# Token transposes on the DMA queue, scales on VectorE, and weights prepared one expert ahead in a fused attention, routing and two-level expert kernel

## Chip, cores and metric

The kernel runs on one core of a Trainium2 chip. The metric is device time in microseconds, the median of several executions; lower is better. TensorE multiplies and transposes through PSUM, VectorE (DVE) and ScalarE (ACT) read PSUM and SBUF, GpSimd (POOL) issues the gathers and scatters, and SyncE (SP) issues the other DMAs.

## What is computed

```python
def _attn_ref(r, k, v, w, u):                      # 4 batches, 8 heads, 768 steps, head size 48
    for t in range(S):
        cur = np.einsum('bhd,bhe->bhde', u[None] * kt, vt)
        y[:, :, t] = np.einsum('bhd,bhde->bhe', rt, state + cur)
        state = w[None, :, :, None] * state + np.einsum('bhd,bhe->bhde', kt, vt)

def _moe_ref(x, w_gate, w1, w2):                   # x 3072x384, 8 experts, F = 1024
    # each token goes to one expert, best logit first, at most 384 tokens per expert
    h = np.maximum(x[mask] @ w1[e], 0.0)
    out[mask] = h @ w2[e]

def _moe2_ref(x, w1, w2, w3, w_out):               # 384 -> 768 -> 384
    h = np.maximum(np.maximum(x @ w1, x @ w2), x @ w3)
    return h @ w_out
```

The attention's output, 3072 rows of 384, is routed, goes through the chosen expert's two matrices, and then through the second layer, whose four matrices arrive as 64-bit floats.

## The kernel before

The kernel has three stages, one behind the other on every engine. The instructions of an engine stand in the order in which the program is written; nothing is reordered.

The attention (class `Attention`) runs 24 steps of 128 tokens. The routing (class `Routing`) is three rounds of a threshold search, `settle`, which writes the row numbers `ids`, a first gather of token rows by POOL, and a branch (`tc.If` at L1297) to a fallback that isn't taken. The experts' stage (`Experts.run`) follows.

For each expert there are 384 tokens in three groups of 128, and four products, each with operands split into a high and a low f16 part, so that every block is three matmuls. `first` makes the hidden layer (8 blocks of 9 matmuls), `second` the expert's output (3 blocks of 24), `third` the second layer's three branches (6 groups of 27) and `fourth` the final product (3 blocks of 18). Each matmul has 384 columns. `turn` transposes the gathered tokens: nine f32 transposes on TensorE into PSUM (L786), after which ACT writes the high part (L798) and DVE the low part (L799).

Weights are prepared beside this by a feed (`Feed`), a list of small items with estimated costs. A matrix of an expert (`weight(e, 0)` or `weight(e, 1)`) is loaded in two blocks of 768 KB, looked at (four sums of squares on ACT, L569), scaled, and split into high parts (ACT, L612) and low parts (DVE, L615). A 64-bit matrix (`double(i)`: 0, 1 and 2 are the layer's branches, 3 is its output matrix) comes in three blocks; for each of these its words are put together on DVE (L657, L658, L665, L672) before the looks and the splits (L693, L696). A load waits for one of four slots, in the order of the list.

A scale is one power of two per matrix. `Scales.spread` gets it from a column of 128 maxima in two items: `turn` transposes the column on TensorE (L395) and reduces the row on DVE (L397), and `share` multiplies the result by a row of ones on TensorE (L401), from whose PSUM tile `powering` works out the scale in some five small DVE operations.

In the attention the feed holds both matrices of experts 0 and 1 and the doubles 0 and 1, spread evenly over the steps (costs 9.0 and 9.3 for an expert's two matrices and 14.8 for a double: 66.2 in all). After it comes a second feed: double 2, then the matrices of expert 2, double 3, and the rest. In the experts' stage `side(time)` runs items at a pace worked out from what is left and when it is due, and `flush(tag)` runs all that are still missing up to a tag.

The order of the products before is: first 0, second 0, first 1, second 1, and then for each expert e `third(e)` with `first(e + 2)` and `turn(e + 3)` between its groups, `second(e + 2)` ahead of its last group, and `fourth(e)`. So the first layer runs two experts ahead of the second.

Of the kernel before, what the change touches and what calls it, by code (L numbers as in the profile page):

```python
# [22 lines left out]
DM = H * D  # L23
# [354 lines left out]
class Scales:  # L378


    def __init__(self, tc, pool, K):
        self.nc, self.pool, self.K, self.n, self.psum = tc.nc, pool, K, 0, None
# [5 lines left out]
    def spread(self, peak, then):  # L388
# [15 lines left out]
        return [turn, share]  # L404

# [53 lines left out]
class Feed:  # L459


    SLOTS, AHEAD = 4, 6
# [53 lines left out]
    def take(self, tag, budget, slot=None, time=1.0, apart=1.0):  # L516
# [3 lines left out]
        while self.left(tag) and self.spare > 0.3:  # L520
            pe = self.items[self.at][2]
            if pe and (self.now < self.ready or slot not in (None, pe)):
# [11 lines left out]
class Experts:  # L534
# [4 lines left out]
    def __init__(self, ctx, tc, K, w1, w2, vs, wo, x_dram, out):  # L539
# [4 lines left out]
        self.fix = ctx.enter_context(tc.tile_pool(name="fixed", bufs=1))  # L544
        self.sc = Scales(tc, ctx.enter_context(tc.tile_pool(name="scales", bufs=1)), K)
# [16 lines left out]
    def peak(self, x):  # L562
        p = self.sc.tile()
        self.nc.vector.tensor_reduce(p, x, AX.X, OP.max)
        return p

# [3 lines left out]

    def weight(self, e, which):

        nc = self.nc
        st = {}
# [16 lines left out]
        def peak():  # L591
            st["peak"] = self.peak(st["peaks"])

        def scale(top):
            st["s"], st["f"] = self.sc.power(top, 3, square=True)
# [11 lines left out]

        def split(n):
            def go():
                if n < len(parts):  # L610
                    raw, (hi, _) = part(*parts[n])
                    nc.scalar.activation(hi, raw, AF.Copy, scale=st["s"])  # L612
                if n:
                    raw, (hi, lo) = part(*parts[n - 1])
                    nc.vector.scalar_tensor_tensor(lo, raw, st["s"], hi, op0=OP.mult, op1=OP.subtract)  # L615
# [5 lines left out]
        turn, share = self.sc.spread(lambda: st["peak"], scale)  # L621
        return ([(look(j), False, [blocks[j // 2]], 0.9) for j in range(4)] + [(peak, False, blocks, 0.2)]
                + [(turn, 4, blocks, 0.2), (share, 2, blocks, 0.8)]
                + [(split(n), False, uses(n), 0.6 + 0.3 * which) for n in range(len(parts) + 1)])

    def double(self, i):
# [6 lines left out]
        st, bits = {}, {}  # L633
# [7 lines left out]
        def magnitude(j):  # L641
            a = bits[j] = self.wp.tile([128, 768], I32, name="da", bufs=2)
            nc.scalar.activation(a.bitcast(F32), pair(j)[1].bitcast(F32), AF.Abs, scale=65536.0)
# [5 lines left out]
        def shift(j):  # L649
            def go():  # L650
                total(j - 1)
                if j == 0:
                    magnitude(0)
                    st["x"] = self.room(i)
                    st["peaks"] = self.fix.tile([128, nb], F32, name=f"peaks{i}")
                x = bits[j].bitcast(F32)
                nc.vector.tensor_scalar(x, x, 2.0, None, op0=OP.max)  # L657
# [3 lines left out]
        def low(j):  # L661
            def go():
                if j + 1 < nb:
# [12 lines left out]
        def last():  # L676
            total(nb - 1)

        def peak():
            st["peak"] = self.peak(st["peaks"])  # L680

        def scale(top):
            st["s"], f = self.sc.power(top, 2, square=True, field=self.vf[:, i:i + 1] if i < 3 else None)
            if i == 3:
                self.wof = f
# [13 lines left out]
        turn, share = self.sc.spread(lambda: st["peak"], scale)  # L699
        near = [[blocks[j]] + blocks[j + 1:j + 2] for j in range(nb)]  # L700
        return ([(f(j), False, b, 1.1) for j in range(nb)
                 for f, b in ((shift, blocks[j:j + 1]), (low, near[j]), (sign, blocks[j:j + 1]))]
                + [(last, False, [], 0.1), (peak, False, [], 0.2), (turn, 4, [], 0.2), (share, 2, [], 0.8)]
                + [(split(j), False, [], 0.9) for j in range(nb + 1)])

# [5 lines left out]
    def common(self):  # L711
# [6 lines left out]
        self.vlow, self.ratio = low, [s[:, i:i + 1].bitcast(F32) for i in range(3)]  # L718

# [54 lines left out]
    def turn(self, e, blocks=False):  # L774
# [6 lines left out]

        def flip(n):
            ps = self.psum.tile([128, CAP], F32, name="px", bufs=3)
            for m in range(3):
                a, j = (n, m) if blocks else (m, n)
                nc.tensor.transpose(ps[:, m * 128:(m + 1) * 128], self.XG[e % 2][a][:, j * 128:(j + 1) * 128], K.identf)  # L786
            tiles.append(ps)

        if blocks:
            flip(0)  # L790
        for n in range(3):
            if n + blocks < 3:
                flip(n + blocks)
            ps = tiles[n]
            hi, lo = (xt[:, t, :, n * 128:(n + 1) * 128] if blocks else xt[:, t, n] for t in range(2))
            if blocks:
                ps = ps.rearrange("p (j n) -> p j n", j=3)
# [40 lines left out]
    def second(self, e, between=lambda j: None):  # L838
# [10 lines left out]
        pk = sc.tile()  # L849
        nc.vector.tensor_reduce(pk, part, AX.X, OP.max)  # L850

        def halve(top):
            s, f = sc.power(top, 3)
# [531 lines left out]
```

## Time and profile before

| | us |
|---|---|
| median of 3 runs | 733.47 |
| lowest and highest | 732.11 to 737.27 |
| profiled execution, its own time | 732.94 |
| span of the profiled execution | 731.2 |
| TensorE busy | 680.0 (93%) |
| VectorE busy | 411.7 (56%) |
| ScalarE busy | 322.1 (44%) |
| GpSimd busy | 238.6 (33%) |

The span runs from the first to the last instruction of the one execution that was profiled; what lies around it is 732.94 - 731.2 = 1.74 us. Busy shares are means over stages with different limits: the attention ends at about 193 us, the routing at about 230 us, and the experts' stage fills the rest.

### The profile page before, as it was taken

The page shows a single profiled execution, that of the slowest core. Times are in us where ns is not written, and L with a number is a line of the kernel's source. Part 1 is how long each engine was busy: PE and PEld are TensorE (multiplying, and loading weights), DVE is VectorE, ACT ScalarE, POOL GpSimd, SP SyncE. Part 2 cuts the span into 40 slices and gives each one's busy share as a digit, 9 for nine tenths or more (in the row PEclk, how much of TensorE's full clock was granted, in tenths as well). Part 3 has the DMA queues.
Part 4 walks back from the last instruction along what each step waited for, and adds up shares of the span by engine and source line. Part 5 has one row for each costly group of instructions (what it writes and reads, how often), then busy time and mean ns, then how long its engine had stood idle before and what let it go on. Part 6 is the DMA issues. An engine that isn't in the chain of part 4 may idle for free.

```text
span 731.2 us, 14572 instructions
## 1 busy us (share of the span) xinstructions
PE 680.0 (93%) x5891; PEld 456.6 (62%) x5891; DVE 411.7 (56%) x954; ACT 322.1 (44%) x657; POOL 238.6 (33%) x264
## 2 busy tenths in 40 slices
PE   5898888999748999999999999999999999999996
PEld 4687667788636755555665666666566665666663
DVE  6779989788673767865453453453535344332120
ACT  3454343454313576655553554544555343232221
POOL 5889777787004200210220220221121021121222
PEclk8999998799756999999999999999999999999999
DMA  5976745562404222421230230321202000000000
GB/s 157 308 230 194 241 138 181 187 199 72 151 1 134 90 85 86 162 87 44 77 119 12 109 118 1 112 83 44 91 30 87 0 33 1 1 34 1 33 1 32
DMA packets 37962, 68.86 MB, mean 94 GB/s; under 512 B 4608, under 2 KB 25216, under 8 KB 37888
## 3 DMA queue, kind: packets, MB, share of 16 engines
q1 hardware_dynamic: 34816, 58.42, 25.0%
q0 software_dynamic: 3072, 9.44, 3.8%
q8 instruction: 48, 0.79, 0.4%
q14 instruction: 26, 0.21, 0.1%
HBM read 58.41 MB, written 9.44 MB: 93 GB/s over the span
## 4 chain that ended last, share of the span: by engine, by line
PE 61%; DVE 3%; issue 2%; ACT 1%; DMA 1%; POOL 1%; POOLq 0%; ACTq 0%; DVEq 0%
PE pg L807 28%; PE ps L807 22%; PE px L893 8%; PE px L401 1%; DVE w L615 1%; PE px L786 1%; DMA stage<-in_moe_w_out_dram 1%; ACT w L612 0%; DVE xt L799 0%; DVE top L877 0%; PE px L395 0%; POOL out_dram L898 0%; DVE x2s L857 0%; POOL gt L880 0%; DVE ht L835 0%
## 5 line engine op out<-in xcount | busy, mean ns | idle before, releaser
L807 PE MATMUL pg<-x2s,v 128*128 128x384 f16 x1296 | 216.8, 326 | 0.0
L807 PEld LDWEIGHTS <-v 128*128 128x128 f16 x1296 | 126.5, 98 | 83.2
L807 PEld LDWEIGHTS <-w 128*128 128x128 f16 x1242 | 115.7, 98 | 70.9 <-issue 1.9
L880 POOL TENSOR_TENSOR gt<-top,gt 128x384 f16<-128x384 f32 x48 | 45.6, 951 | 342.4 <-ACT gt L879 301.5
L877 DVE SCALAR_TENSOR_TENSOR top<-pg,sc,top 128x384 f32<-128x384 f32 x96 | 59.3, 618 | 125.4 <-PE pg L807 122.9
L807 PE MATMUL ps<-ht,w 128*128 128x384 f16 x576 | 95.6, 326 | 0.0
L807 PE MATMUL ps<-xt,w 128*128 128x384 f16 (+1 forms) x540 | 88.5, 317 | 0.8 <-DVE ht L835 0.6
L879 ACT ACTIVATE gt<-top 128x384 f16<-128x384 f32 x48 | 25.1, 523 | 139.3 <-DVE top L877 139.3
L615 DVE SCALAR_TENSOR_TENSOR w<-stage,sc,w 128x512 f16<-128x512 f32 (+1 forms) x80 | 74.2, 950 | 7.4 <-ACT w L612 7.3
L893 PE MATMUL px<-wo,gt 128*128 128x384 f16 x432 | 72.6, 326 | 0.0
L612 ACT ACTIVATE w<-stage,sc 128x512 f16<-128x512 f32 (+1 forms) x80 | 60.8, 797 | 9.6 <-DVE sc L430 9.2
L893 PEld LDWEIGHTS <-gt 128*128 128x128 f16 x432 | 41.8, 98 | 27.0
L569 ACT ACTIVATE junk<-stage 128x768 bf16<-128x768 f32 x64 | 53.4, 835 | 2.8 <-DMA stage<-in_moe_w_dram 2.2
L835 DVE SCALAR_TENSOR_TENSOR ht<-ps,ht 128x384 f16<-128x384 f32 x56 | 30.6, 554 | 32.6 <-ACT ht L834 32.6
L263 ACT ACTIVATE junk<-x 128x384 bf16<-128x384 f32 x24 | 12.6, 523 | 69.5 <-DVE x L262 67.7
L847 DVE TENSOR_REDUCE part<-ps 128x1 f32<-128x384 f32 x24 | 13.4, 556 | 51.4 <-ACT x L846 51.4
L226 PE MATMUL pA<-rt,kt 64*128 64x128 f32 x384 | 34.3, 314 | 7.8 <-DVE am L229 7.5
L898 POOL DMA_INDIRECT out_dram<-o,ids x24 | 23.4, 974 | 44.6 <-ACT o L896 44.6
L226 PEld LDWEIGHTS pA<-rt,kt 64*128 64x128 f32 x384 | 28.4, 212 | 14.3 <-DVE am L229 9.8
L229 DVE TENSOR_TENSOR am<-pA,mask 128x512 f32<-128x512 f32 x48 | 30.7, 680 | 8.9 <-PE pA L226 8.9
L875 ACT ACTIVATE top<-pg,sc 128x384 f32<-128x384 f32 x48 | 27.8, 579 | 16.6 <-PE pg L807 16.2
L202 POOL TENSOR_TENSOR bv<-v,bon 128x384 f32<-128x384 f32 x24 | 23.1, 964 | 31.0 <-DVE bon L200 28.5
(229 smaller groups left out, 916.8 us busy)
## 6 DMA issues: line engine op xcount, KB each, us to landing
stage<-in_moe_w_dram SPq DMA_DIRECT2D x41, 768.0 KB, 4.9
kn<-in_k_dram SPq DMA_DIRECT2D x24, 192.0 KB, 4.6
rn<-in_r_dram SPq DMA_DIRECT2D x24, 192.0 KB, 4.1
v<-in_v_dram SPq DMA_DIRECT2D x24, 192.0 KB, 3.1
rt<-in_rt_dram SPq DMA_DIRECT2D x48, 96.0 KB, 3.2
x_rows<-x SPq DMA_DIRECT2D x24, 192.0 KB, 2.6
stage<-in_moe_w_out_dram SPq DMA_DIRECT2D x3, 768.0 KB, 4.1
xg<-x_rows,ids POOLq DMA_INDIRECT x24, 4.6
```

Of the source, the lines that this page charges most:

```text
L226: nc.tensor.matmul(pa[s][:, j, :], kt[FULL[s], j * C:(j + 1) * C], rt[FULL[s], j * C:(j + 1) * C], start=True, stop=True, skip_group_check ...
L229: nc.vector.tensor_mul(am[:, s], pa[s], self.mask[:, None, :].to_broadcast([128, NP, C]))
L569: self.nc.scalar.activation(self.K.junk, x, AF.Square, accum_out=total)
L612: nc.scalar.activation(hi, raw, AF.Copy, scale=st["s"])
L615: nc.vector.scalar_tensor_tensor(lo, raw, st["s"], hi, op0=OP.mult, op1=OP.subtract)
L807: nc.tensor.matmul(p[:, rows], w[:, wi, k, cols], x[:, xi, k, rows], start=k == 0 and wi + xi == 0, stop=k == kb - 1 and xi == 1, skip_gro ...
L835: nc.vector.scalar_tensor_tensor(h[:, 1, f], p, 0.0, h[:, 0, f], op0=OP.max, op1=OP.subtract)
L875: nc.scalar.activation(t, p, AF.Copy, scale=self.ratio[i])
L877: nc.vector.scalar_tensor_tensor(t, p, self.ratio[i], top, op0=OP.mult, op1=OP.max)
L879: nc.scalar.activation(gt[:, 0, g], top, AF.Copy)
L880: nc.gpsimd.tensor_sub(gt[:, 1, g], top, gt[:, 0, g])
L893: nc.tensor.matmul(p, gt[:, gi, g, a * 128:(a + 1) * 128], self.WO[:, wi, g, :], start=g == 0 and gi + wi == 0, stop=g == self.KG - 1 and ...
```

## The change

Four things change.

1. `Scales.around` replaces `spread` in the experts' stage: the column is transposed on DVE in four 32x32 blocks, reduced, turned back with a broadcast, and copied twice; no TensorE instruction is left in it. In the attention the old way stays (`early`).
2. `turn` of experts 1 to 7 splits the gathered rows first, from SBUF, on ACT and DVE, and three transposing DMAs on SP's queue (`dma_start_transpose`, one for each group of 128 tokens, 192 KB) bring high and low parts into place. Expert 0 keeps the nine transposes on TensorE.
3. In the loop over experts `third(e)` now has `first(e + 1)` and `second(e + 1)` in it, and for e = 0 none; due times follow. Double 3 is due before `fourth(0)`, which now comes directly behind `third(0)`.
4. `weight(1, 1)` leaves the attention's feed (56.9 is left of 66.2) and opens the second feed. Its four looks run in the first two rounds of the routing, its scale behind the first gather, and its splits in the experts' stage. `Feed.chain` puts the looks (or the words) of the next matrix ahead of, or between, the scale and splits of the one before.

```diff
+    def around(self, peak, powers, kind):
...
+        def collect():
+            peak(a[:, :1])
+            for q in range(4):
+                nc.vector.transpose(b[:32, 32 * q:32 * q + 32], a[32 * q:32 * q + 32])
+            nc.vector.tensor_reduce(c[:32, :1], b[:32], AX.X, OP.max)
+
+        def share():
+            nc.vector.transpose(d[:32], c[:32, :1].to_broadcast([32, 32]))
+            nc.vector.tensor_copy(d[32:64, :1], d[:32, :1])
+            nc.vector.tensor_copy(d[64:, :1], d[:64, :1])
...
+    def chain(self, parts):
+
+        parts = [(tag, [(tag,) + x for x in items], at) for tag, items, at in parts]
+        for n, (tag, items, at) in enumerate(parts):
+            cut = next(m for m, x in enumerate(items) if x[2])
+            parts[n] = (items[:cut], items[cut:], at)
+        self.plan += parts[0][0]
+        for n, (_, tail, at) in enumerate(parts):
+            at = len(tail) if at is None else at
+            self.plan += tail[:at] + (parts[n + 1][0] if n + 1 < len(parts) else []) + tail[at:]
...
+    def aside(self, pieces):
+
+        for _ in range(pieces):
+            self.feed.run()
...
-        for i in late:
-            feed.add(1, self.double(i))
-        feed.add(1, [(self.common, False, [], 1.5)], 0)
+        self.early = False
+        parts = [(0.2, self.weight(1, 1), None)] + [(1, self.double(i), 0) for i in late]
+        parts[-1] = (1, parts[-1][1] + [(self.common, False, [], 1.5)], 0)
+        parts.append((1.5, self.double(3), 0))
         for e in range(2, E):
-            for which in range(2):
-                feed.add(e + 0.3 * which, self.weight(e, which))
-            if e == 2:
-                feed.add(2.5, self.double(3))
+            parts += [(e, self.weight(e, 0), 7), (e + 0.3, self.weight(e, 1), 6)]
+        feed.chain(parts)
...
+        if not blocks:
+            for a in range(3):
+                t = self.act.tile([128, 2, DM], F16, name="xr", bufs=3)
+                nc.scalar.activation(t[:, 0], self.XG[e % 2][a], AF.Copy, scale=K.xs)
+                nc.vector.scalar_tensor_tensor(t[:, 1], self.XG[e % 2][a], K.xs, t[:, 0], op0=OP.mult, op1=OP.subtract)
+                nc.sync.dma_start_transpose(xt.rearrange("p t j n -> p (t j) n")[:, :, a * 128:(a + 1) * 128],
+                                            t.rearrange("p t n -> p (t n)"))
+                yield
+            return
...
-            n = e + 2
+            n = e + 1
             third, fourth = self.third(e, 0, self.KG), self.fourth(e)
-            first = self.first(n) if n < E else iter(())
-            flush(n)
+            first = self.first(n) if e and n < E else iter(())
+            if e:
+                flush(n)
...
+        self.aside((2, 2, 0)[n])
...
         then()
         for _ in other:
             pass
+        aside(3)
...
-    for which in range(2):
-        feed.add(0, X.weight(1, which))
+    feed.add(0, X.weight(1, 0))
```

What this does to the order shows on three engines. First SP's queue of loads, around the branch behind the routing, before (`stage` is a slot of weights; those of 128x1536 are the blocks of double 2, `flag` is the branch's condition):

```order
L269 DMA x_rows<-x 128x384 x5
L556 DMA stage<-in_moe_w_dram 128x1536 x3
L1222 TENSOR_LOAD flag
L1222 ISA x2
L1297 COMPARE_AND_BRANCH
```

and SP behind the branch now, from the end of the branch on (`xr` are a group's split rows, `xt` the transposed tokens):

```order
L1394 UNCONDITIONAL_BRANCH x2
L872 DMA_TRANSPOSE xt<-xr 128x6x128 x3
L599 DMA stage<-in_moe_w_dram 128x1536 x2
L599 DMA stage<-in_moe_w_out_dram 128x2x768 x3
L599 DMA stage<-in_moe_w_dram 128x3x512 x2
L872 DMA_TRANSPOSE xt<-xr 128x6x128 x3
```

Two of double 2's three blocks moved from ahead of the branch to behind expert 1's three transposes, and the blocks of double 3 (`in_moe_w_out_dram`) now come directly behind them.

Second VectorE in `first` of expert 1, before (`ht` is the low part of a hidden block, `sc` and `vf` scales, `wo` the scratch of double 2's words, `v_86` its split):

```order
L835 SCALAR_TENSOR_TENSOR ht<-ps,ht 128x384
L835 SCALAR_TENSOR_TENSOR ht<-pg,ht 128x384
L416 TENSOR_SCALAR sc_4729<-px 128x1
L423 TENSOR_SCALAR sc_4732<-sc_4729 128x1
L425 TENSOR_SCALAR sc_4732<-sc_4732 128x1
L430 TENSOR_SCALAR sc_4731<-sc_4732 128x1
L430 TENSOR_SCALAR vf<-sc_4732 128x1
L696 SCALAR_TENSOR_TENSOR v_86<-wo,sc_4731,v_86 128x768
L835 SCALAR_TENSOR_TENSOR ht<-ps,ht 128x384
L696 SCALAR_TENSOR_TENSOR v_86<-wo,sc_4731,v_86 128x768
L835 SCALAR_TENSOR_TENSOR ht<-pg,ht 128x384
L696 SCALAR_TENSOR_TENSOR v_86<-wo,sc_4731,v_86 128x768
```

and VectorE in the same product now (`da` and `gt` are the words of double 3, `x2s` the low part of expert 0's output):

```order
L926 SCALAR_TENSOR_TENSOR ht<-ps,ht 128x384
L732 TENSOR_SCALAR da<-da 128x768
L733 TENSOR_SCALAR da<-da 128x768
L954 SCALAR_TENSOR_TENSOR x2s<-x_4570,sc_4743,x2s 128x384
L926 SCALAR_TENSOR_TENSOR ht<-pg,ht 128x384
L742 SCALAR_TENSOR_TENSOR da<-stage,da 128x768
L954 SCALAR_TENSOR_TENSOR x2s<-x_4570,sc_4743,x2s 128x384
L926 SCALAR_TENSOR_TENSOR ht<-pg,ht 128x384
L749 SCALAR_TENSOR_TENSOR gt<-stage,da 128x768
L954 SCALAR_TENSOR_TENSOR x2s<-x_4570,sc_4743,x2s 128x384
L926 SCALAR_TENSOR_TENSOR ht<-ps,ht 128x384
L732 TENSOR_SCALAR da<-da 128x768
```

The words of double 3 moved from `second(1)` and `third(0)` into `first(1)`, and the splits of double 2 moved out of it, into the last blocks of `second(1)`.

Third ScalarE at the start of `third(0)`, before (`x_4858` is expert 1's output, `junk,wpeak` a look at a matrix, `top` the branch maximum that empties PSUM, `da` a word of double 3, `w_5066` expert 2's second matrix):

```order
L846 ACTIVATE x_4858<-ps 128x384
L569 ACTIVATE junk,wpeak_4803<-stage 128x768 x2
L643 ACTIVATE da<-stage 128x768
L846 ACTIVATE x_4858<-ps 128x384
L643 ACTIVATE da<-stage 128x768
L875 ACTIVATE top_5023<-pg,sc_4771 128x384
L879 ACTIVATE gt<-top_5047 128x384
L612 ACTIVATE w_5066<-stage,sc_5059 128x768 x3
```

and ScalarE at the same place now (`x_4844` is expert 1's output, `wo` the high part of double 3):

```order
L937 ACTIVATE x_4844<-ps 128x384 x2
L774 ACTIVATE v_86<-wo,sc_4886 128x768 x3
L937 ACTIVATE x_4844<-ps 128x384
L607 ACTIVATE junk,wpeak_4960<-stage 128x768 x4
L971 ACTIVATE top_4976<-pg,sc_4929 128x384
L975 ACTIVATE gt<-top_5000 128x384
L971 ACTIVATE top_5038<-pg,sc_4929 128x384
L975 ACTIVATE gt<-top_5062 128x384
L774 ACTIVATE wo<-gt,sc_5021 128x768 x3
L870 ACTIVATE xr<-xg_2854,sc_2965 128x384
L870 ACTIVATE xr<-xg_2855,sc_2965 128x384
L870 ACTIVATE xr<-xg_2856,sc_2965 128x384
```

Four looks, at expert 2's first matrix, now stand directly ahead of the first evacuation of `third(0)`, where a word of double 3 stood, and three splits of double 3 and three of tokens between its second and its third group.

## Rows read from the trace of the kernel before

**Rows 1.** Busy us (instructions) of PE, PEld, DVE, ACT, POOL by stretch; clock, DMA, GB/s.
```profile
247.60:286.10 38.50, 37.78 (x236) 22.95 (x235) 29.07 (x68) 26.90 (x54) 3.87 (x3) 1.00 0.32 99
286.10:324.50 38.40, 36.80 (x227) 22.01 (x226) 29.01 (x61) 21.39 (x41) 7.08 (x7) 1.00 0.42 138
324.50:711.40 386.90, 386.90 (x2391) 234.34 (x2390) 163.07 (x373) 167.83 (x322) 72.05 (x93) 1.00 0.15 49
```

**Rows 2.** The chain that ended last, its last TensorE piece (start us, us, what).
```profile
689.41 21.95 PE pg L807 x135
```

**Rows 3.** Timeline of TensorE: expert 1's transposes, and one scale.
```profile
246.53 1.15 PE L786 MATMUL px<-identf,xg 128*128 128x128 f32 x9
247.51 11.86 PE L807 MATMUL ps<-ht,w 128*128 128x384 f16 x72
259.30 0.27 PE L395 MATMUL px<-identf,sc 128*1 128x128 f32 x1
259.41 1.62 PE L807 MATMUL ps<-xt,w 128*128 128x384 f16 x9
...
262.43 0.38 PE L401 MATMUL px<-sc,onesf 1*128 1x1 f32 x2
262.74 1.64 PE L807 MATMUL ps<-xt,w 128*128 128x384 f16 x9
```

**Rows 4.** Groups by line and shape, TensorE, 230 us to the end.
```profile
L786 PE MATMUL px<-identf,xg 128*128 128x128 f32 x72 | 10.3, 287 | 3.3 <-PEq L1297 1.4 <-issue 1.1 <-DVE sc L416 0.9
L401 PE MATMUL px<-sc,onesf 1*128 1x1 f32 x44 | 8.3, 256 | 0.7 <-DVE xt L799 0.7
```

**Rows 5.** Groups by line and shape, VectorE, 247.6 to 286.1 us.
```profile
L615 DVE SCALAR_TENSOR_TENSOR w<-stage,sc,w 128x512 f16<-128x512 f32 x6 | 4.1, 748 | 0.7 <-ACT w L612 0.7
L799 DVE SCALAR_TENSOR_TENSOR xt<-px,sc,xt 128x384 f16<-128x384 f32 x6 | 3.3, 611 | 0.0
...
L672 DVE SCALAR_TENSOR_TENSOR wo<-stage,da 128x768 int32<-128x768 int32 x3 | 2.9, 951 | 0.0
...
L665 DVE SCALAR_TENSOR_TENSOR da<-stage,da 128x768 int32<-128x768 int32 x2 | 1.9, 952 | 0.0
...
L658 DVE TENSOR_SCALAR da<-da 128x768 int32<-128x768 int32 x2 | 1.1, 560 | 0.1
L657 DVE TENSOR_SCALAR da<-da 128x768 f32<-128x768 f32 x2 | 1.1, 552 | 0.0
...
L423 DVE TENSOR_SCALAR sc<-sc 128x1 int32<-128x1 int32 x2 | 0.3, 154 | 0.1
```

**Rows 6.** The same for 230 to 720 us: the splits of an expert's second matrix.
```profile
L615 DVE SCALAR_TENSOR_TENSOR w<-stage,sc,w 128x768 f16<-128x768 f32 x24 | 24.4, 1021 | 3.8 <-ACT w L612 3.8
```

**Rows 7.** Timeline of TensorE in the attention: the start of three steps.
```profile
72.79 0.66 PE L212 MATMUL pT<-identf,kp 128*128 128x128 f32 x4
...
78.99 0.66 PE L212 MATMUL pT<-identf,kp 128*128 128x128 f32 x4
...
89.42 0.66 PE L212 MATMUL pT<-identf,kp 128*128 128x128 f32 x4
```

**Rows 8.** Timeline of the attention's end: the last rows `x`.
```profile
187.24 2.88 DVE L615 SCALAR_TENSOR_TENSOR w<-stage,sc,w 128x768 f16<-128x768 f32 x3 [0.64 <-ACT w L612]
187.49 1.15 PE L247 MATMUL pY<-v,am 128*64 128x64 f32 x32
...
190.03 0.62 DVE L262 TENSOR_TENSOR x<-pY,bv 128x192 f32<-128x192 f32 x2
```

**Rows 9.** DMA issues: tensors, count, KB each, median us from issue to landing.
```profile
stage<-in_moe_w_dram SPq DMA_DIRECT2D x41, 768.0 KB, 4.9
...
x_rows<-x SPq DMA_DIRECT2D x24, 192.0 KB, 2.6
```

**Rows 10.** Timeline around the branch: the end of the routing, the next gather.
```profile
224.86 0.18 DVE L1221 TENSOR_SCALAR ids<-pn 128x24 int32<-128x24 f32 x1 [0.29 <-PE pn L1219]
...
229.35 0.94 POOL L770 DMA_INDIRECT xg<-x_rows,ids  x1 [0.33 <-DVEq L1297]
```

More of the change, by code (lines that the diff above doesn't have):

```diff
@@ L521, in take @@
             pe = self.items[self.at][2]
[L522 removed]
+            if isinstance(pe, dict):
+                if self.now < pe["sent"] + self.LAG:
+                    return
+            elif pe and (self.now < self.ready or slot not in (None, pe)):
                 return
@@ L560, in block, with scaled, peak, then @@
         return b
[L562 to L565, printed above, removed]
     def square(self, x, total):
         self.nc.scalar.activation(self.K.junk, x, AF.Square, accum_out=total)
+    def scaled(self, st, column, powers, blocks):
+        if self.early:
+            def peak():
+                st["m"] = self.sc.tile()
+                column(st["m"])
+            def then(top):
+                for _ in powers(top):
+                    pass
+            turn, share = self.sc.spread(lambda: st["m"], then)
+            return [(peak, False, blocks, 0.2), (turn, 4, blocks, 0.2), (share, 2, blocks, 0.8)]
+        collect, share, end = self.sc.around(column, powers, "weights")
+        def done():
+            end()
+            self.mark(st)
+        return [(collect, st, blocks, 1.2), (share, False, blocks, 0.6), (done, False, blocks, 0.8)]
+    def mark(self, st):
+        st["sent"] = self.feed.now
     def weight(self, e, which):
         nc = self.nc
-        st = {}
+        st = {"sent": 0.0}
         if which == 0:
@@ L619, in uses @@
             return [blocks[parts[i][0]] for i in (n - 1, n) if 0 <= i < len(parts)]
[L621 to L624, printed above, removed]
+        looks = [(look(j), False, [blocks[j // 2]], 0.9) for j in range(4)]
+        return (looks + self.scaled(st, column, powers, blocks)
+                + [(split(n), st if n == 0 and not self.early else False, uses(n), 0.6 + 0.3 * which)
+                   for n in range(len(parts) + 1)])
     def double(self, i):
@@ L656, in go @@
                 x = bits[j].bitcast(F32)
+                if not early and j + 1 < nb:
+                    magnitude(j + 1)
                 nc.vector.tensor_scalar(x, x, 2.0, None, op0=OP.max)
@@ L677, in last, with column, powers @@
             total(nb - 1)
[L679 to L683, printed above, removed]
+            if not early:
+                self.mark(st)
+        def column(out):
+            nc.vector.tensor_reduce(out, st["peaks"], AX.X, OP.max)
+        def powers(top):
+            if i < 3:
+                st["f"] = self.vf[:, i:i + 1]
+            yield from self.sc.powering(top, 2, True, st)
             if i == 3:
-                self.wof = f
+                self.wof = st["f"]
         def halves(j):
@@ L697, in split @@
             return go
-        turn, share = self.sc.spread(lambda: st["peak"], scale)
         near = [[blocks[j]] + blocks[j + 1:j + 2] for j in range(nb)]
[L701 to L704, printed above, removed]
+        return ([(lambda: magnitude(0), False, blocks[:1], 0.3)] * (not early)
+                + [(f(j), False, b, 1.1) for j in range(nb)
+                   for f, b in ((shift, blocks[j:j + 1] if early else near[j]), (low, near[j]), (sign, blocks[j:j + 1]))]
+                + [(last, False, [], 0.1)] + self.scaled(st, column, powers, [])
+                + [(split(j), st if j == 0 and not early else False, [], 0.9) for j in range(nb + 1)])
     def room(self, i):
@@ L981, in run @@
             next(third)
+            step()
             side(G1)
-            flush(n + 0.3)
-            soon = self.second(n, lambda j: side(F2)) if n < E else [lambda: None] * 2
+            if e and n < E:
+                flush(n + 0.3)
+                soon = self.second(n, lambda j: side(F2))
+                step()
             next(third)
-            soon[0]()
+            step()
             side(G1)
-            flush(2.5)
-            next(fourth)
-            soon[1]()
-            side(G2)
-            for _ in range(2):
+            flush(1.5)
+            for a in range(3):
                 next(fourth)
+                step()
+                step()
                 side(G2)
@@ L1282, in exact, with run @@
         nc.vector.tensor_add(self.nl, self.nl, on)
-    def run(self, ctx, other, scales, then):
+    def run(self, ctx, other, aside, scales, then):
         tc = self.tc
-        self.other = other
+        self.other, self.aside = other, aside
         self.work = ctx.enter_context(tc.tile_pool(name="rwork", bufs=2))
@@ L1337, in body @@
     with ExitStack() as rctx:
-        routing.run(rctx, X.inputs(), X.sc, lambda: X.gather(0))
+        routing.run(rctx, X.inputs(), X.aside, X.sc, lambda: X.gather(0))
     X.open(ctx)
```

131 lines of the change are left out of this document (75 added, 56 removed).

## The prediction

> **What bounds the kernel now.** I read the busy time by stretch first, then the chain that ended last, then the timelines of the places that the change touches. In the long stretch from 324.5 us to 711.4 us TensorE is busy for all of 386.9 us [rows 1]; VectorE has 163.1 us of work there and ScalarE 167.8 us, so neither bounds it. The chain of the same stretch is TensorE's matmuls end to end: its last piece is 135 matmuls in 21.95 us, 0.1626 us each [rows 2]. The 2391 instructions of that stretch are 2304 matmuls of this kind, 36 transposes of tokens and 17 scales of three instructions. 2304 x 0.1626 = 374.6; what is left, 12.3 us, is what the change can take there.
>
> Ahead of it the picture differs. From 247.6 us to 286.1 us, while `second(0)`, `first(1)` and `second(1)` run, VectorE is busy for 29.1 of 38.5 us [rows 1], and from 286.1 us to 324.5 us for 29.0 of 38.4 us, with TensorE idle for 1.6 us. Here VectorE has little room, and the change moves work into exactly this part. The attention is a loop whose usual step takes 72.79 to 78.99 = 6.2 us and whose heavy ones, with the words of a double on VectorE, take 78.99 to 89.42 = 10.4 us [rows 7].
>
> **TensorE's part.** Nine transposes keep the next matmul from 246.53 to 247.51, that is 0.98 us [rows 3]. There are 72 in the trace [rows 4]; those of expert 0 stay, 63 go: 7 x 0.98 = 6.9 us. A scale costs TensorE 259.30 to 259.41 = 0.11 us for the transpose and 262.43 to 262.74 = 0.31 us for the pair that shares it [rows 3]; 44 such instructions [rows 4] are 22 scales: 22 x 0.42 = 9.2 us. Together 16.1 us, all on the path where TensorE is never idle, and nothing on TensorE comes in their place. Two idle stretches go with them if nothing else is late: 0.7 us before 286.1 and 1.6 us behind [rows 1].
>
> **VectorE from 247.6 us on.** Why I don't book these 16 us in full. The stretch before `third(0)` has 29.1 us of work on VectorE now. The change adds: the four splits of expert 1's second matrix, 4 x 1.02 = 4.1 [rows 6]; the words of double 3, which now stand in `first(1)`, three blocks of 0.55 + 0.56 + 0.95 + 0.95 = 3.0, so 9.0 [rows 5]; three operations on the first block of double 2, which ran before 247.6 and now can't, 2.1; and two scales the new way, each some seven more operations of 0.15 [rows 5], 2.0. The block of 2.1 is late because the routing's `aside` pays the feed's budget in advance: seven items, cost 6.2, are charged before `side` first runs, so it starts nothing in `first(0)`. What leaves the stretch are the tokens of expert 2, 3 x 0.61 = 1.8, the six splits of expert 2's first matrix, 4.1 [rows 5], and that matrix's scale, about 1.1. Sum: 29.1 + 4.1 + 9.0 + 2.1 + 2.0 - 1.8 - 4.1 - 1.1 = 39.3 us. TensorE alone would reach `third(0)` about 281.6, as three products of 72 x 0.1626 = 11.7 follow 246.5. VectorE can't be through before 247.6 + 39.3 = 286.9, and the branch 2 of the second layer that `third(0)` needs now stands behind the words of double 3. With all of the 9.4 us in which VectorE waits in that stretch today it would be 296.3. I take half of these waits, 291.6, since ScalarE holds it up in places that the order shows: a hidden block of `first(1)` is emptied on ScalarE only behind looks and words whose data VectorE has yet to make.
>
> **`third(0)` and `fourth(0)`.** They are 162 + 54 matmuls, 35.1 us. In front of the first evacuation ScalarE now has four looks, and between the second and the third group both engines have three splits of double 3 and three of tokens. PSUM holds three blocks for these groups, 3 x 1.46 us of matmuls; three splits of 1.02 and three of 0.61 are 4.9 us on VectorE beside the group's own work, so TensorE waits there. I take 6 us for all such waits, with bounds of 0 (they fit into the slack) and 9.4 (as much as VectorE waited in the stretch before). End of `fourth(0)`: 291.6 + 35.1 + 6 = 332.7.
>
> **The rest.** Behind it stand third and fourth of seven experts, first and second of six: 2376 matmuls. The chain leaves TensorE 81 before the end, so 2295 x 0.1626 = 373.2. Transposes and scales are gone; 12.3 less 36 x 0.109 and 17 x 0.42 leaves 1.3 us of idle time today, which I keep. The tail from 711.4 to the span's end, 19.8, stays. 332.7 + 373.2 + 1.3 + 19.8 = 727.0. VectorE has room for the longer scales there: 163 of 387 us [rows 1].
>
> **The attention.** At its end the last rows `x` wait on VectorE behind the splits of the matrix that moves: TensorE is done at 188.64, the addition starts at 190.03 [rows 8], 1.4 us. Else VectorE loses four splits and a scale, 3.8 + 1.1 us (2.88 / 3 = 0.96 each [rows 8]), but in steps that have their usual length already; the gain comes from spreading what remains more thinly, cost 56.9 for 66.2 over the same steps, which relieves the 10.4 us steps. Between 0 and 4.9 us; I take 2.9. Sum 4.3.
>
> **The routing.** The two pairs of looks lie on ScalarE where it waits for the next round; the scale's 16 small operations, some 2.7 us, run from 225.04, when VectorE is done, to about 227.8, and the branch lets POOL go on at 229.35 [rows 10]. Nothing, and 1 us if that cover is short.
>
> **The transposing DMAs.** No row shows one. Each moves 192 KB, as the store of `x_rows` does, which lands in 2.6 us [rows 9]. The three of expert 1 are issued near 249.3, and `first(1)` needs them at about 258.3; but behind them on SP's queue stands the second block of double 2, which ScalarE wants near 255 and which itself takes 4.9 us [rows 9]. From below, they overlap and cost nothing; from above, three in a row at 4.9 each hold the block back by 14.7. I take 1.5, near the store's row. For the other experts there are tens of microseconds.
>
> The Trainium skill has a rule against this edit: in VectorE: DVE Perf Modes, section The three transpose paths, a 128x128 transpose of two-byte data takes 390 ns on TensorE and 1309 ns by DMA, so the DMA is named only where the result must not go to PSUM. The trace has 0.109 us for one of the f32 transposes on TensorE, less than the page; no run here shows the DMA's. By the page a group of expert 1 is 18 x 1.309 = 23.6 us if they run one by one, an estimate; the sum would then be some 18 us higher.
>
> **Sum.** 727.0 - 4.3 + 1.5 = 724.2 us of span, against 731.2. With the 1.74 us around it 725.9, against 732.94 of its own; the median lies 0.5 us above that execution, so 726.4.
>
> **Rivals.**
> 1. VectorE's waits vanish. If the feed's items fall into gaps, `third(0)` starts at 286.9 and its own waits are nil: 4.7 + 6 less, and no cost of the DMA, 1.5: 714.2. For it: the later stretch has VectorE at 42% busy without a wait. Against it: 39.3 of 39.3 us would have to run without one gap, where today 9.4 of 38.5 are gaps.
> 2. The transposes hold SP's queue. Double 2's second block comes 14.7 us later; of this the 4.7 us of waits that I book already are part: 726.4 - 1.5 + 14.7 - 4.7 = 734.9, slower than now. It decides once the three take more than about 14 us to leave the queue. For it: one queue, in order, and no slack on ScalarE. Against it: 192 KB lands in 2.6 us.
> 3. VectorE gives back everything: all waits stay (296.3, so 4.7 more), and the attention gains its tail alone, 2.9 less: 734.0, no difference that can be told.
>
> **How the numbers follow.** The forecast has 0.40, with 720 to 732 as its own range; rival 1 has 0.22, rival 3 has 0.20, rival 2 has 0.18. About 1% is what a measurement of this kernel can tell from no change, so from 726.1 to 740.8 is the same. Faster is rival 1 and rather over half of the forecast, 0.44; slower is the far part of rival 2 and of unknown stalls, 0.14; the rest, 0.42, is the same. The range reaches from 711, below rival 1, to 741, above rival 2 with the branch's 1 us and more waits.
>
> **What would show it.** Right: in the profile after, no TensorE row of transposes or scales behind the first expert; `third(0)` starting later against the routing's end than today's 286.1 - 230 = 56 us, with TensorE waiting for VectorE or ScalarE in `first(1)` and in `third(0)`; from `fourth(0)` on matmuls at 0.163 us without a gap; an attention some 4 us shorter. Wrong: a `third(0)` at 282 to 287 us less the attention's gain (rival 1), double 2's words waiting for a DMA (rival 2), or gaps on TensorE later, in which it waits for a scale's VectorE chain or for transposed tokens.

## The result and the profile after

The changed kernel takes 726.04 us (median of 4 runs, 724.14 to 728.44); the kernel before took 735.37 us in the runs taken with them (4 runs, 732.11 to 737.86). The ratio is 0.9896, with an interval of 0.9851 to 0.9941: faster by 1.0%. 726.4 was forecast. The span of the profiled execution is 724.8 us, its own time 726.55 us. Ratios are of fast runs alone; of all runs in this document that leaves out two, 735.48 and 736.81 us, of the kernel called matrix back in attention. The forecast sum holds to 0.6 us, but four of its terms do not; they cancel.

The page's busy times of the kernel after, TensorE's granted clock in 40 slices (in tenths of full speed: its two levels are 2.4 GHz, full speed, and 1.2 GHz, half of it, and a value between is a mean over both), and the DMA packets:

```profile
PE 661.6 (91%) x5759; PEld 440.4 (61%) x5759; DVE 442.2 (61%) x1117; ACT 321.3 (44%) x657; POOL 240.0 (33%) x264
...
PEclk8999989999558999999999999999999999999999
...
DMA packets 54762, 72.98 MB, mean 101 GB/s; under 512 B 21408, under 2 KB 42016, under 8 KB 54688
```

TensorE lost 18.4 of 680.0 us, the span 6.4 us.

Busy time by stretch, columns as in [rows 1]. First the attention of the kernel before, which ends at 193.35 us:

```profile
0.00:193.35 193.35, 167.29 (x2669) 139.25 (x2669) 156.83 (x302) 86.47 (x182) 140.75 (x143) 0.91 0.58 184
```

and of the kernel after: the attention, the routing, `second(0)` to `third(0)`, `third(0)` with `fourth(0)`, and the rest:

```profile
0.00:183.13 183.13, 160.87 (x2666) 133.96 (x2666) 153.16 (x292) 79.44 (x170) 141.88 (x143) 0.94 0.58 186
183.13:221.54 38.41, 21.80 (x114) 16.57 (x115) 26.42 (x146) 12.59 (x47) 4.26 (x4) 0.54 0.21 70
237.49:287.62 50.13, 39.10 (x217) 22.25 (x216) 38.19 (x81) 25.03 (x45) 0.00 (x0) 0.93 0.40 122
287.62:331.03 43.41, 37.42 (x219) 21.66 (x217) 29.26 (x92) 23.94 (x46) 12.07 (x14) 0.96 0.36 92
331.03:724.80 393.77, 386.61 (x2377) 232.22 (x2375) 189.74 (x499) 175.14 (x339) 76.09 (x97) 1.00 0.22 63
```

The attention has practically the same 2669 TensorE instructions; they take 6.4 us less, at a mean granted clock of 0.94 for 0.91, and TensorE's idle time falls from 26.1 to 22.3 us. The two stretches behind the first expert, each 216 matmuls (35.1 us at 0.1626 [rows 2]), have TensorE busy for 39.1 and 37.4 us, at 0.93 and 0.96 of the clock, and idle for 11.0 and 6.0 us. The rest is matmuls end to end.

TensorE's timeline there ([rows 3] is the same place before; in brackets the idle time in front and who ended it). Of the kernel before first the routing's and the first transposes' start:

```profile
193.35 1.17 PE L1084 MATMUL pn<-identf,raw 128*96 128x128 f32 x4 [0.42 <-ACT raw L352]
...
230.11 1.51 PE L786 MATMUL px<-identf,xg 128*128 128x128 f32 x6 [1.44 <-PEq L1297]
```

After:

```profile
183.13 1.17 PE L1178 MATMUL pn<-identf,raw 128*96 128x128 f32 x4 [0.42 <-ACT raw L352]
...
221.54 1.51 PE L880 MATMUL px<-identf,xg 128*128 128x128 f32 x6 [3.63 <-DVEq L1394]
...
237.49 11.86 PE L898 MATMUL ps<-ht,w 128*128 128x384 f16 x72
251.12 1.62 PE L898 MATMUL ps<-xt,w 128*128 128x384 f16 x9 [1.77 <-DVE part L938]
...
256.50 1.62 PE L898 MATMUL ps<-xt,w 128*128 128x384 f16 x9 [2.29 <-DVE part L938]
...
264.43 2.51 PE L898 MATMUL ps<-xt,w 128*128 128x384 f16 x9 [3.39 <-DVE ht L926]
266.73 2.46 PE L898 MATMUL pg<-xt,w 128*128 128x384 f16 x9
269.03 1.63 PE L898 MATMUL ps<-xt,w 128*128 128x384 f16 x9
274.24 13.54 PE L898 MATMUL ps<-ht,w 128*128 128x384 f16 x72 [3.58 <-ACT junk L607]
287.62 4.55 PE L898 MATMUL pg<-x2s,v 128*128 128x384 f16 x27
292.56 8.94 PE L898 MATMUL pg<-x2s,v 128*128 128x384 f16 x54 [0.39 <-ACT top L971]
304.10 9.17 PE L898 MATMUL pg<-x2s,v 128*128 128x384 f16 x54 [2.60 <-ACT top L971]
316.19 6.22 PE L898 MATMUL pg<-x2s,v 128*128 128x384 f16 x27 [2.93 <-ACT top L971]
...
331.03 4.55 PE L898 MATMUL pg<-x2s,v 128*128 128x384 f16 x27
```

Some of these waits are paid twice. Behind the 3.39 us, nine matmuls take 2.51 us and the next nine 2.46 instead of 1.63, at a mean clock of 0.63. Behind the 3.58 us, 72 take 13.54 us instead of 11.86, and from 276 to 278 us the clock is 0.50, the lower level. Behind the 2.93 us, 27 take 6.22 instead of 4.55. Behind the 1.77 and the 2.29 us nothing is lost: nine matmuls take 1.62. The branch, released by TensorE's sequencer before, is now released by VectorE's queue.

The piece of the chain that ended last in which `second(0)` hands over to the words of double 2:

```profile
242.11 0.57 DVE part L938
242.68 0.78 SPq L872
243.50 5.69 DMA stage<-in_moe_w_dram
249.21 0.89 ACT da L714
250.10 0.39 ACT x L937
```

and SP's queue, with the new operation's row among the DMA issues behind it (answering to [rows 9]):

```profile
239.47 3.99 SPq L872 DMA_TRANSPOSE xt<-xr  x3
243.50 1.73 SPq L599 DMA_DIRECT2D stage<-in_moe_w_dram  x2
```

```profile
xt<-xr SPq DMA_TRANSPOSE x21, 4.2
```

and ScalarE's word of double 2 that waits for the load:

```profile
249.21 0.89 ACT L714 ACTIVATE da<-stage 128x768 f32<-128x768 f32 x1 [3.04 <-DMA stage<-in_moe_w_dram]
```

The chain runs through a load that stands behind the three transposes. The evacuation of `second(0)`'s second block (ScalarE, `x` at 250.10) stands behind the word that waits for the load, so TensorE, whose next block needs the space in PSUM, stops at 249.35 (251.12 - 1.77).

### The profile page after: what moved, and what is told of

The parts are those of the page before. It is cut to its first block, busy times and chain, and to the rows that moved or that the text cites. A ratio compares the mean times of both kernels' runs of the same rounds, so it can differ in the third digit from the quotient of the medians.

```text
span 724.8 us, 14507 instructions
## 1 busy us (share of the span) xinstructions
PE 661.6 (91%) x5759; PEld 440.4 (61%) x5759; DVE 442.2 (61%) x1117; ACT 321.3 (44%) x657; POOL 240.0 (33%) x264
## 2 busy tenths in 40 slices
DMA packets 54762, 72.98 MB, mean 101 GB/s; under 512 B 21408, under 2 KB 42016, under 8 KB 54688
## 4 chain that ended last, share of the span: by engine, by line
PE 55%; DVE 5%; issue 4%; DMA 2%; ACT 1%; POOL 1%; POOLq 0%; SPq 0%; DVEq 0%; ACTq 0%
PE pg L898 26%; PE ps L898 21%; PE px L989 8%; DMA stage<-in_moe_w_dram 2%; DVE top L973 1%; DVE da L742 1%; ACT junk L607 1%; POOL gt L976 1%; DVE sc L420 0%; DVE wo L749 0%; DVE ht L926 0%; DVE wo L777 0%; DVE da L732 0%; POOL out_dram L994 0%; DVE da L733 0%
## 5 line engine op out<-in xcount | busy, mean ns | idle before, releaser
L898 PE MATMUL pg<-x2s,v 128*128 128x384 f16 x1296 | 219.1, 328 | 6.0 <-ACT top L971 5.9
L898 PEld LDWEIGHTS <-w 128*128 128x128 f16 x1242 | 119.1, 100 | 85.8 <-issue 15.9
L938 DVE TENSOR_REDUCE part<-ps 128x1 f32<-128x384 f32 x24 | 13.4, 557 | 58.2 <-ACT x L937 58.2
L994 POOL DMA_INDIRECT out_dram<-o,ids x24 | 24.4, 1015 | 41.5 <-ACT o L992 41.5
L226 PE MATMUL pA<-rt,kt 64*128 64x128 f32 x384 | 31.0, 292 | 4.6 <-DVE am L229 4.1
L126 POOL TENSOR_TENSOR rt<-rt,tr 128x512 f32<-128x512 f32 x22 | 32.6, 1480 | 0.9 <-DMA rt<-in_rt_dram 0.9
L202 POOL TENSOR_TENSOR bv<-v,bon 128x384 f32<-128x384 f32 x24 | 24.6, 1027 | 22.6 <-DVE bon L200 22.6
```

The lines of the kernel that those rows point to most:

```text
L126: (engine or self.nc.gpsimd).tensor_mul(self.RT[i], self.RT[i], self.tr)
L226: nc.tensor.matmul(pa[s][:, j, :], kt[FULL[s], j * C:(j + 1) * C], rt[FULL[s], j * C:(j + 1) * C], start=True, stop=True, skip_group_check ...
L898: nc.tensor.matmul(p[:, rows], w[:, wi, k, cols], x[:, xi, k, rows], start=k == 0 and wi + xi == 0, stop=k == kb - 1 and xi == 1, skip_gro ...
```

## Experiments

Each kernel is the changed one with the edit named. Ratios are to the kernel before on the same chip, with 95% intervals. The stretches, in us, come from TensorE's timelines: the attention's end; from there to expert 0's first transposes; `second(0)` to `third(0)`; `third(0)` to `third(1)`, so with `fourth(0)`; the rest to the span's end.

| kernel | ratio | attention | routing | second(0) to third(0) | third(0), fourth(0) | rest |
|---|---|---|---|---|---|---|
| changed | 0.9896 (0.9851 to 0.9941) | 183.1 | 38.4 | 50.1 | 43.4 | 393.8 |
| scales on TensorE | 1.0002 (0.9979 to 1.0025) | 185.2 | 38.5 | 51.6 | 42.4 | 400.9 |
| tokens on TensorE | 0.9923 (0.9898 to 0.9949) | 182.5 | 38.5 | 45.7 | 42.9 | 398.2 |
| matrix back in attention | 0.9942 (0.9906 to 0.9979) | 197.4 | 36.8 | 47.8 | 40.2 | 393.3 |
| block ahead | 0.9846 (0.9795 to 0.9896) | 183.2 | 38.6 | 45.7 | 42.2 | 393.7 |
| budget not prepaid | 0.9821 (0.9779 to 0.9863) | 182.7 | 38.3 | 46.9 | 40.0 | 393.8 |
| double 3 behind double 2 | 0.9823 (0.9762 to 0.9884) | 181.8 | 38.3 | 44.7 | 46.0 | 393.8 |
| scale behind the branch | 0.9877 (0.9822 to 0.9932) | 183.1 | 36.7 | 50.2 | 42.0 | 393.8 |
| the last three together | 0.9777 (0.9727 to 0.9827) | 183.8 | 36.9 | 41.9 | 42.8 | 393.7 |
| and tokens of expert 2 later | 0.9777 (0.9728 to 0.9826) | 180.3 | 37.5 | 42.6 | 42.2 | 394.8 |
| and looks later | 0.9766 (0.9713 to 0.9819) | 184.3 | 36.6 | 41.8 | 41.8 | 393.8 |
| both of these | 0.9735 (0.9686 to 0.9784) | 184.2 | 37.4 | 41.5 | 40.2 | 394.3 |

Each stretch is read from one profiled execution. Where an edit doesn't touch a stretch, it can come back the same or not: with the scale behind the branch, `second(0)` to `third(0)` is 50.2 us for 50.1, but `third(0)` with `fourth(0)` 42.0 for 43.4, so a difference of 1.4 us there tells nothing. Of the single edits only that of the scales has an interval clear of the changed kernel's.

**What the saved TensorE work is worth.** Two runs put one part each back.

```diff
-        if self.early:
+        self.calls = getattr(self, "calls", 0) + (not self.early)
+        if self.calls != 1:
...
-        return sc.around(column, powers, "layer") + [halve(j) for j in range(self.KD)]
+        m = sc.pool.tile([128, 1], F32, name="scm", bufs=2)
+        return ([lambda: column(m)] + sc.spread(m, lambda top: [None for _ in powers(top)])
+                + [halve(j) for j in range(self.KD)])
```

> Only the scales of the experts' stage go back to TensorE (a transpose and a pair each, 21 of the 22; the one that the routing holds stays on VectorE). Theory A, what TensorE no longer does is saved in full wherever it never waits: some 17 of them lie behind third(0), 17 x 0.42 = 7.1 us, so this kernel is 6 to 8 us slower than the changed one from fourth(0) on, near the time of the kernel before. Rival B, TensorE had other waits there that the scales filled: the stretch behind fourth(0) grows by less than 2 us. Rival C, the long chain on VectorE is what holds up the stage from second(0) to third(0): then third(0) starts 2 us or more sooner here, and the net is +4 us or less.

The rest grew from 393.8 to 400.9 us, 7.1, as theory A has it. The last stretch of this kernel, beside the one of the changed kernel above:

```profile
333.44:734.30 400.86, 394.09 (x2425) 237.45 (x2424) 169.06 (x388) 176.65 (x339) 76.55 (x97) 1.00 0.22 62
```

It has 48 more TensorE instructions (16 scales of three), 7.5 us more of work, and about the same idle time (6.8 us for 7.2). C falls: `second(0)` to `third(0)` is 1.5 us longer, not shorter. The time is that of the kernel before.

```diff
-        if not blocks:
+        if not blocks and False:
             for a in range(3):
...
-            for j in range(3):
-                nc.tensor.transpose(ps[:, j * 128:(j + 1) * 128], self.XG[e % 2][n][:, j * 128:(j + 1) * 128], K.identf)
+            for m in range(3):
+                a, j = (n, m) if blocks else (m, n)
+                nc.tensor.transpose(ps[:, m * 128:(m + 1) * 128], self.XG[e % 2][a][:, j * 128:(j + 1) * 128], K.identf)
...
```

> Only the token transposes of experts 1 to 7 go back to TensorE (nine f32 transposes per expert, split from PSUM). Theory A: six groups behind third(0) cost 6 x 0.98 = 5.9 us there, and the group of expert 1 another 1 us ahead of second(0): 6 to 7 us slower than the changed kernel. Rival C, the three transposes at the head of SP's queue are what delays double 2's second block (ScalarE waited 3.04 us for it): without them that wait is gone, third(0) starts 2 to 3 us sooner and the net is +4 us. Against C: the load also waits for a slot that VectorE's splits of expert 1's second matrix free, and if these decide, ScalarE's wait stays.

Both are there, with other sizes than expected: the rest is 4.4 us longer (five groups, 0.89 each), and `second(0)` to `third(0)` is 4.5 us shorter. In the profile the two cancel; in the ratios 2 us are left (0.9923 against 0.9896), with intervals that overlap. So the DMA transposes as placed earn little.

**SP's queue.** One load is issued earlier and nothing else moves:

```diff
+        feed.ahead()
         go(self.turn(1))
         soon = self.second(0, lambda j: side(F2))
```

> One row of SP's queue moves: the load of double 2's second block is issued ahead of expert 1's three transposing DMAs, not behind them. Theory C, the transposes wait on SP for VectorE's low parts until 239.5 us and the load behind them has had its slot since long before: ScalarE's wait of 3.04 us for the block goes, second(0) to third(0) is 3 to 4.5 us shorter (50.1 us in the changed kernel, 45.7 with the tokens on TensorE), and the kernel is 3 to 5 us faster than the changed one. Rival F, the tokens' experiment gained its 4.5 us because VectorE and ScalarE no longer split the tokens between the last evacuations of first(0) and second(0): then less than 1.5 us here.

C is shown for the stretch, and F falls: it takes 45.66 us, what the tokens' experiment had. SP's queue, the two stretches of this kernel and `second(1)` on TensorE's timeline:

```profile
180.56 31.00 SPq L599 DMA_DIRECT2D stage<-in_moe_w_dram  x4
239.70 3.99 SPq L872 DMA_TRANSPOSE xt<-xr  x3
```

```profile
237.72:283.38 45.66, 37.33 (x218) 21.57 (x217) 38.13 (x81) 24.82 (x45) 0.00 (x0) 0.96 0.39 117
283.38:325.62 42.24, 37.44 (x218) 21.63 (x217) 29.02 (x91) 23.92 (x46) 12.08 (x14) 0.96 0.38 91
```

```profile
271.68 11.86 PE L898 MATMUL ps<-ht,w 128*128 128x384 f16 x72 [3.48 <-ACT junk L607]
```

The block's load is issued by 211.6 us (180.56 + 31.00), not at 243.5, and ScalarE no longer waits for it. Of the 4.5 us, TensorE's idle time gives 2.7 (11.0 to 8.3) and its own work 1.8 (39.1 to 37.3), at a clock of 0.96 for 0.93. The 72 matmuls of `second(1)`, behind a wait of 3.48 us, take 11.86 us here and took 13.54 behind 3.58 us; that this part follows from the load isn't shown. By the ratios the gain is 3.7 us (0.0050 of 733.5), with intervals that overlap.

**The attention.**

```diff
-        parts = [(0.2, self.weight(1, 1), None)] + [(1, self.double(i), 0) for i in late]
+        parts = [(1, self.double(i), 0) for i in late]
...
-        self.aside((2, 2, 0)[n])
...
-        aside(3)
...
-    feed.add(0, X.weight(1, 0))
+    for which in range(2):
+        feed.add(0, X.weight(1, which))
```

> Only expert 1's second matrix goes back into the attention's feed; the routing then holds none of its items. Theory A, the attention became 10 us shorter because its feed is spread more thinly: here it ends at about 193 us again, the routing is 1.6 us shorter, and third(0) starts 4 to 8 us sooner after the routing, as 4.1 us of splits and a scale are gone from VectorE: net -1 to +5 us against the changed kernel. Rival D, the attention gained from elsewhere: it still ends at 183 to 186 us and the net is -5 us or better.

```profile
0.00:197.41 197.41, 174.28 (x2669) 144.57 (x2670) 156.78 (x303) 86.72 (x182) 138.88 (x143) 0.87 0.57 180
```

For the attention theory A holds, and more than it asked: it is 14.3 us longer than in the changed kernel, of which 13.4 us are TensorE's own time for the same instructions, at 0.87 of the clock, and 0.9 us its idle time. VectorE's work grew by only 3.6 us. This attention is that of the kernel before, whose profile has 193.35 us, so some 4 us of it vary between executions. The one without the matrix stands in the profiles of the changed kernel and of its ten other variants: 180.3 to 185.2 us, with 158.1 to 163.3 us of TensorE's time. So that the matrix costs the attention 8 us or more is shown. Why TensorE takes longer for it, when its idle time hardly differs, is not. Behind the attention the routing is 1.6, `second(0)` to `third(0)` 2.3 (4 to 8 were expected) and `third(0)` with `fourth(0)` 3.2 us shorter; the net of the ratios is +0.5%, some 3 us, with intervals that overlap.

**The order of VectorE's work.** Three edits, and then all of them:

```diff
         first = self.first(0, True, 5)
+        feed.spare = 0.0
```

> Only the feed's budget is set to zero where the experts' stage begins, so that the items which the routing ran are not charged against first(0). Theory A, VectorE is idle in first(0) (1.79, 0.91, 0.91, 0.91 us) while 4 splits and a block of words wait for budget: they start there, the slots come free sooner, double 2's second block is loaded ahead of the transposes, and third(0) starts 3 to 6 us sooner: 3 to 6 us faster than the changed kernel. Rival E, VectorE's work in the stage is what counts, and it is only put in another order or lengthens second(0)'s own evacuations: less than 1.5 us either way.

Theory A fits: 5.5 us by the ratios (0.0075 of 733.5), 7.0 in the profile, 3.2 of it in `second(0)` to `third(0)` and 3.4 behind. But this edit also puts the block's load ahead of the transposes, so the two gains are not separate.

```diff
-        parts = [(0.2, self.weight(1, 1), None)] + [(1, self.double(i), 0) for i in late]
-        parts[-1] = (1, parts[-1][1] + [(self.common, False, [], 1.5)], 0)
+        parts = [(0.2, self.weight(1, 1), None)] + [(1, self.double(i), None) for i in late]
+        parts[-1] = (1, parts[-1][1] + [(self.common, False, [], 1.5)], None)
```

> The words of double 3 stand behind double 2's scale and splits in the feed, no longer ahead of them. Theory A, 9.0 us of words on VectorE stand between what the branch 2 of third(0) needs and its data: third(0) starts 4 to 8 us sooner (50.1 us from second(0) now); the words then run in third(0) and fourth(0), whose 43.4 us grow by 2 to 5 us, for double 3 must be complete ahead of fourth(0). Net 0 to 5 us faster than the changed kernel. Rival G, the words only move: third(0) and fourth(0) lose all that the start gains, or more, and the net is -1 to +4 us.

`third(0)` starts 5.5 us sooner after `second(0)`, and the stretch behind it is 2.6 us longer, as theory A has it; the ratio says some 5 us, of which the profile puts 1.3 into the attention, which the edit doesn't touch.

```diff
-        aside(3)
         self.aside = lambda pieces: None
         with tc.If(bad != 0) as _:
             self.more(self.MORE)
             then()
+        aside(3)
```

> The three pieces of the scale that VectorE runs between the routing's ids and the branch are put behind the branch. Theory H, the branch is released by VectorE's queue, and 2.7 us of small operations stand in front of it: routing's start to the first transposes of expert 0 is 36.8 us again, as in the kernel before, not 38.4, and TensorE's clock falls for less of first(0): 1.5 to 2.5 us faster than the changed kernel. Rival I, the branch waits for the first gather or TensorE's sequencer anyway: 38.4 stays and the time too.

```profile
219.72 1.51 PE L880 MATMUL px<-identf,xg 128*128 128x128 f32 x6 [2.48 <-PEq L1393]
```

H holds for the stretch: 36.7 us, and the branch is released by TensorE's sequencer again, as before. What H expected of `first(0)` did not come: from the first transposes to `second(0)` it is 16.2 us here and 15.95 in the changed kernel. The gain of 1.4 us in the whole is within the intervals.

> Three edits of this study together: the budget isn't prepaid, the words of double 3 stand behind double 2's splits, and the scale's pieces stand behind the branch. If the three give-backs are separate, the gains add: 720 less 1.6 for the branch less 0 to 4 for the order, 714 to 719 us. If the order only moves the words into third(0), 718 to 722 us.

The ratio is 0.9777 (718.22 us), some 8.7 us below the changed kernel's and with an interval clear of it, in the range in which the gains partly add. Two more edits were then tried on top of these:

```diff
-                    go(self.turn(e + 2))
+                    if e:
+                        go(self.turn(e + 2))
...
                 next(fourth)
+                if a == 0 and e == 0:
+                    go(self.turn(2))
```

> The three edits together, and in addition the tokens of expert 2 are split inside fourth(0), not between the second and third groups of third(0). Theory J, the 2.6 us for which TensorE waits there for ScalarE are the tokens' 1.6 us and double 3's splits ahead of the evacuation: third(0) to the end of fourth(0) is 1.5 to 2.5 us shorter than 42.8 us: 716 us. Rival K, the splits of double 3 alone hold it, or first(2) then waits for its tokens: within 1 us of 718.2.

Rival K holds: 42.2 us for 42.8, and the same ratio; the median is lower (716.27 us), but so is that of the kernel before in these runs, 731.35 us against 734.42.

```diff
-        parts.append((1.5, self.double(3), 0))
+        parts.append((1.5, self.double(3), 3))
```

> The three edits together, and in addition the four looks at expert 2's first matrix stand behind double 3's scale, not ahead of it. Theory J, they are what ScalarE does for 3 us ahead of third(0)'s first evacuation: the wait of 1.2 us there goes and VectorE's 3.96 us of idleness is used: 1 to 3 us shorter. Rival K, the looks only move to a place where they hold another evacuation, and the matrix is late at first(2): -1 to +3 us.

The wait of 1.2 us in front of the second group went, and the 2.6 us later stayed (2.67). The stretch is 1.0 us shorter, which can't be told from chance, in the stretch or in the whole.

> Both further edits on the three. If each removes its own wait, 714 to 716 us; if the same evacuations wait for the next piece of work in line, as VectorE and ScalarE have as much to do as before, 717 to 719 us.

Together they take 40.2 us for 42.8, at a clock of 1.00 (the second line):

```profile
237.93:279.40 41.47, 36.70 (x218) 21.53 (x217) 37.15 (x83) 22.38 (x41) 0.00 (x0) 0.96 0.47 130
279.40:319.56 40.16, 35.91 (x218) 21.02 (x216) 28.20 (x79) 24.71 (x48) 10.14 (x13) 1.00 0.22 64
```

Of the 2.6 us, 1.5 are TensorE's own time (37.4 to 35.9) and 1.1 its idle time. The ratio of 0.9735 (714.09 us) is the best of the study, faster than both kernels; its interval lies below that of the changed kernel but overlaps that of the three edits, so what the last two add is not shown.

## Why the prediction was right, and where it was not

| step | forecast, us | measured, us |
|---|---|---|
| the attention | -4.3 | 183.13 - 193.35 = -10.2 |
| the routing, to the first transposes | 0 | 38.41 - 36.76 = +1.65 |
| first transposes to `second(0)`, expert 1's transposes aside | 0 | 15.95 - (17.40 - 0.98) = -0.5 |
| `second(0)` to `third(0)` | 291.6 - 246.5 + 1.5 = 46.6 | 50.1 |
| `third(0)` and `fourth(0)` | 41.1 | 43.4 |
| the rest and the tail | 394.3 | 393.8 |

**TensorE's part** is right: 7.1 us for the scales and 4.4 us for five groups of tokens came back in the rest when they were put back.

**VectorE from 247.6 us on** is right in its size: 39.3 us of work were summed up, 38.2 measured. Where the block is loaded ahead, `second(0)` to `third(0)` takes 45.66 us, against 45.1 without the DMA in the forecast; of these 8.3 us are TensorE's idle time (10.0 by the forecast, 45.1 - 35.1) and 2.2 us its own time beyond 35.1, so the agreement is partly luck. That VectorE's order makes the stretch long, as the prediction argued, is shown: with double 3's words behind double 2's splits it is 44.7 us, though the block is still loaded behind the transposes there.

**The transposing DMAs** were mis-sized: 1.5 us taken, 4.5 measured. The prediction counted how long three of them hold the queue once they are issued. That is 3.99 us. But the first also waits at the head of SP's queue for VectorE's low parts, until 239.47 us (the prediction had them issued near 249.3), and the load behind had its slot by 211.6. So rival 2 is real in its mechanism, and one of the prediction's signs of being wrong, double 2's words waiting for a DMA, came; its size is far from the 14.7 us. Of the 4.5, 1.8 us are TensorE's own time, as said above. Here the Trainium skill's rule (VectorE: DVE Perf Modes, The three transpose paths) has the direction: the nine f32 transposes of a group cost TensorE 0.98 us, while one of its three DMAs, six blocks of two-byte data, lands in 4.2 us, 0.70 us a block by division. The 1.309 us a block, one by one, that the Trainium skill's page has is not what was seen. Behind 331 us, with the tokens of experts 2 to 7, TensorE waits once, 0.4 us, for another thing.

**`third(0)` and `fourth(0)`**: 6 us of waits forecast, 6.0 measured. The 2.3 us that are missing are TensorE's own time, 37.4 us for 35.1, at 0.96 of the clock: the sum counted the waits and every matmul at 0.1626 us. The same holds ahead of it, 39.1 for 35.1. No run gives the order of the products (the third change) back by itself, so its part in these waits is argued.

**The attention** was mis-sized by the same step, with the other sign: TensorE's idle time fell by 3.8 us (4.3 forecast), and its instructions took 6.4 us less, at a higher clock. The prediction read the matrix's price from VectorE's operations alone, 3.8 + 1.1 us, and took 4.9 as its upper bound, 6.3 with the tail. That bound was wrong: 10.2 us were measured.

**The routing** was to be covered; it wasn't. VectorE starts the scale's operations 1.2 us after `ids` (214.62 us) and is done at 218.57, and TensorE then comes out of the branch behind VectorE's queue, idle for 3.63 us (1.44 before). The stretch grew by 1.65 us, against a bound of 1, and that is gone where the operations stand behind the branch.

So 726.4 was right by its sum, and that is luck: -5.9 us in the attention, and -0.5 in each of two other rows, against +3.5, +2.3 and +1.65. The mechanisms that it named were there, but the steps that priced the attention, the DMA and the routing, and every matmul at full clock, were wrong in size. Rival 1 did not come. Of rival 3 the first half came in its number: `second(0)` to `third(0)` took 50.1 us, where all waits kept would be 296.3 - 246.5 = 49.8; but 4.5 us of it go with the DMA. Its second half did not come: the attention gained far more than its tail.

## What to carry to other kernels

Where waits are moved, price a TensorE stretch twice: the idle time, and the matmuls behind it, at full clock and at the clock that a row with such waits shows, for not every wait here was followed by a lower one. A DMA that waits for a late producer can hold up a load behind it on its queue, however short it is itself, as here from 211.6 to 243.5 us: issue the loads that are ready first, and look at what stands behind a new entry. A feed that pays in advance for work done elsewhere leaves the next stage's idle slots empty, as `first(0)` had them here.

## What was not expected of the hardware

Practically the same 2669 attention instructions took TensorE 167.3 and 174.3 us with one matrix more beside them, at a mean clock of 0.91 and 0.87, and 158.1 to 163.3 us without it, at 0.93 to 0.99. The 21 transposing DMAs brought packets under 512 B to 21408; 37962 packets in all before became 54762, 800 for each of them. A scale on VectorE takes 2.7 us, since its small operations are chained, each some 0.15 to 0.2 us long; the four 32x32 transposes alone are 0.84 us.
